# Third visit's keys and queries by DMA transposes, two score runs joined, and other places for copies and exponentials

## The chip, the cores and the metric

The kernel runs on one core of one Trainium2 chip. The metric is the device time of one execution in microseconds (us). The core has five engines that each work through their own instructions in order: TensorE (matmuls, PE in the profile; its weight loads are PEld), VectorE (DVE), ScalarE (ACT), GpSimd (POOL) and SyncE (SP, which here only issues DMAs). They wait for one another through semaphores.

## The reference

Attention in a sliding window, then a two-layer network on its output.

```python
scores = np.matmul(q, k.transpose(0, 1, 3, 2)) / np.sqrt(D)     # B, H, S, D = 8, 8, 576, 64
scores = np.where(np.abs(pos[:, None] - pos[None, :]) <= 32, scores, -1e9)
attn = softmax(scores)
x = np.matmul(attn, v).transpose(0, 2, 1, 3).reshape(B * S, H * D)   # 4608 x 512
h = x @ w_in                                                          # 512 x 2048
g = h * (1.0 / (1.0 + np.exp(-1.702 * h)))
out = g @ w_out                                                       # 2048 x 512
```

Inputs and output are float32; the kernel computes in bf16 and f16 with sums in float32.

## The kernel before, in words

The 4608 rows are cut into 36 units of 128 queries, and four units make a tile of 512 rows; there are nine tiles, 0 to 8. The queries of a unit are shifted by 32 rows, so that a block of 64 queries meets exactly 128 keys. All the code is written in one order by hand; every engine takes its own instructions from that order.

**A unit** goes through these steps: GpSimd issues the loads of keys, queries (`load_kq`, lines 137 to 143) and values (`load_v`, 208 to 213); keys and queries are transposed, either by TensorE with a copy out of the accumulator (`T_pe`, 242 to 251) or by a DMA that SyncE issues (`T_dma`, 236 to 240, called by `turn`, 811 to 813); `scores` (267 to 284) multiplies in 64x64 parts of the array and takes exponentials on ScalarE; `band` (308) multiplies the mask in on VectorE; `values` (316) multiplies with the values; `norm` (335) divides on VectorE; `x_T` and `x_T2` (385 to 410) transpose the result for layer 1. `odd_v` (218) copies values to a second buffer whose rows are shifted by 64; it runs on GpSimd. There are 9 buffers of values, 5 shifted ones, 5 each of untransposed keys and queries, and 7 each of transposed ones from unit 8 on.

**A tile** then goes through two layers. For tile 0 both are done in the plain way (`layer1_plain`, 477, and `layer2_plain`, 569: 32 matmuls of 512 columns for its first half). The others use Strassen's scheme with seven products (`l1_group`, 512 to 549, four groups a tile, counted 0 to 3; `layer2`, 597), whose sums of weights, inputs and gelus are made by VectorE (`w1_sums`, `w2_sums`, `x_sums`, `g_sums`, `g0_sum`). In `l1_group` the products 1, 7, 6, 2, 5, 4, 3 follow one another; line 537 and line 543 are the two VectorE sums between them that TensorE waits for, line 532 and 533 are the ScalarE copies, and line 524 is the gelu.

**Layer 2 as filler.** Layer 2 of a tile is a list, `self.l2` (also `more`), of single matmuls; `do(list, n)` takes the next n of them. So layer 2 of one tile fills the gaps in layer 1 and in the attention of the next ones. `fill(i)` in `first_layer1` (958 to 981, layer 1 of tile 1) says how many stand behind product i, and how many of the VectorE sums in `dv` are issued there; `side` does the same between products. `l2eng` is the engine that copies finished parts of layer 2's output, `seed2` the one that copies its starting sums.

**The order around the change.** `opening` (662 to 787) does units 0 to 7 and layer 1 of tile 0. The gelu needs another function table on ScalarE than the exponential. In the opening, some results of layer 1 are therefore kept aside by VectorE (`kept`) and their gelus deferred (`later=gelus`); line 743 takes one exponential of a single column, which makes ScalarE load the exponential's table there. Then come `x_sums(1)`, `first_layer1` with the transpose visits of units 8 to 12 (`T_pe` at its groups 1, 2, 3), and in `run` (905 to 947) the attention of units 8 to 15 among the items of layer 2. `back(2)` (847) starts layer 1 of tile 2.

**Queues.** All loads go through GpSimd's queue in order, stores of outputs (line 558) and DMA transposes through SyncE's. An instruction that waits holds up what is behind it on its engine.

Of the kernel before, what the change touches and what calls it, by code (L numbers as in the profile page):

```python
# [26 lines left out]
class _Kernel:  # L27
# [186 lines left out]

    def odd(self, u):
        return self.vo[u % 5 if u < 16 else (2, 3, 4, 0)[u % 4]]
# [14 lines left out]
    def place(self, c, u):  # L231
        t = self.sb(c + "T", [128, 4, 128], BF16, 7)
# [34 lines left out]
    def scores(self, u, tag):  # L267
# [15 lines left out]
        for eo in range(2):  # L283
            self.nc.scalar.activation(p[:, eo].rearrange("k h s -> k (h s)"), sc[eo], AF.Exp, scale=self.scale)  # L284
# [22 lines left out]

    def band(self, u, eng=None):
# [3 lines left out]
        pv = p.rearrange("p e (h b) s -> p (e h) b s", b=2)  # L312
# [41 lines left out]
    def values_four(self, u):  # L354
# [5 lines left out]
        for tag in self.FOUR:  # L360
            lo, n, pad = self.four(tag)
            for i in range(n):
                x, h = divmod(lo + i, self.H)
                at, more = pad + i * (D + 1), pad * (i == 0)
                for blk in range(2):
                    vt = (self.ve[(u + x) % 9], self.odd(u + x))[blk].rearrange("p h d -> p (h d)")
                    self.mm(self.acc[u][tag][64 * blk:64 * blk + 64, at - more:at + D + 1],
                            p[x][:, h % 2, h // 2 * 2 + blk, :], vt[:, h * (D + 2) - more:h * (D + 2) + D + 1],
# [200 lines left out]
    def layer2_plain(self, t, pr):  # L569
# [3 lines left out]
        def part(i, f):  # L573
# [5 lines left out]
            if f == 15:  # L579
                self.copy((self.nc.vector, self.nc.scalar)[i * pr], st["o"][:, i, :], st[i])  # L580
# [81 lines left out]
    def opening(self):  # L662
# [72 lines left out]
        l1(0, 8)  # L735
# [4 lines left out]
        l1(0, 10)  # L740
        l1(1, 8)
        self.T_four("q", "tA", (dve, act))
        act.activation(self.spark, self.spark, AF.Exp)
        gelus = []
        kept = [self.sb("s7", [128, 512], F32, 2)]
        room = self.sb("xs", [128, 2, 512], F32, 1, "room")
        kept += [room[:, i, :] for i in range(2)]
# [147 lines left out]
    def run(self):  # L895
# [20 lines left out]
        do(more, 4)  # L916
# [8 lines left out]
        do(more, 8)  # L925
# [102 lines left out]
```

## Time and profile before

| what | us |
| --- | --- |
| median of 3 runs | 279.58 (279.38 to 279.86) |
| the profiled execution | 279.59 |
| its span, first instruction to last | 277.8 |
| TensorE busy | 266.3 |
| VectorE busy | 212.1 |
| ScalarE busy | 197.3 |
| GpSimd busy | 138.6 |

The granted TensorE clock was 1.0 throughout. The time that runs show is 1.8 us more than the span, which lies ahead of the first instruction and behind the last. In the rows of a timeline stand the start and the duration in us from the span's start, the engine, the line, the operation, its output and inputs, the shape and type, how many instructions were merged (x8), and in brackets how long the engine stood idle before and what released it. Matmuls overlap, so the distance between starts says more than a duration. Line 70 is the helper that issues every matmul and line 67 the one that issues every copy; they are told apart by their tiles: `h` is layer 1, `o` layer 2, `sc` scores, `pv` values, `tp` a transpose. `kst` and `qst` are untransposed keys and queries, `kT` and `qT` transposed ones.

### The profile page before, as it was taken

What the parts mean: (1) busy time and instruction counts of PE and PEld (TensorE: products, weight loads), DVE (VectorE), ACT (ScalarE), POOL (GpSimd) and SP (SyncE); (2) the same over time, 40 slices, a digit from 0 to 9 for tenths busy, and PEclk for the clock granted to TensorE, in tenths of its full rate; (3) what the DMA queues carried; (4) which work ended last, traced back from release to release, by engine and by line L of the source; (5) the groups of instructions that cost most, each with busy time, mean ns of one, the idle gap of its engine ahead of it and who ended that gap; (6) DMA issues with size and microseconds to landing.
All of it is one profiled execution on the core that took longest, in us unless ns stands there. A gap on an engine that the chain in (4) does not pass through costs nothing.

```text
span 277.8 us, 8904 instructions
## 1 busy us (share of the span) xinstructions
PE 266.3 (96%) x3652; PEld 224.8 (81%) x3652; DVE 212.1 (76%) x487; ACT 197.3 (71%) x346; POOL 138.6 (50%) x216
## 2 busy tenths in 40 slices
PE   1989999999999999999999999999999999999994
PEld 1668656888888888888888888888888888888883
DVE  3455898897899788878888887888798878855631
ACT  2586896989896689568966895698569856577420
POOL 8895597999592089729641974294430000000000
PEclk9999999999999999999999999999999999999999
DMA  8999999999999999999999999999992024202033
GB/s 86 166 206 195 178 207 168 170 150 164 139 162 189 155 121 153 174 176 166 188 178 153 130 172 148 163 145 139 136 136 77 2 82 74 76 2 76 2 113 117
DMA packets 150809, 37.74 MB, mean 136 GB/s; under 512 B 138608, under 2 KB 146416, under 8 KB 150768
## 3 DMA queue, kind: packets, MB, share of 16 engines
q0 software_dynamic: 106656, 18.42, 96.4%
q1 hardware_dynamic: 43664, 18.23, 38.0%
q8 instruction: 28, 0.46, 0.7%
q10 hardware_dynamic: 448, 0.52, 0.6%
q14 instruction: 13, 0.11, 0.1%
HBM read 36.83 MB, written 9.44 MB: 167 GB/s over the span
## 4 chain that ended last, share of the span: by engine, by line
PE 91%; DVE 4%; ACT 2%; issue 1%; POOL 1%; POOLq 0%; DVEq 0%
PE o L70 40%; PE h L70 39%; PE sc L70 5%; PE pv L70 4%; PE tp L179 1%; PE tp L203 1%; POOL kq L154 1%; ACT p L284 1%; DVE xn L345 1%; PE tp L409 0%; PE tp L249 0%; DVE b L433 0%; DVE o_sb L67 0%; PE tp L397 0%; ACT kq L67 0%
## 5 line engine op out<-in xcount | busy, mean ns | idle before, releaser
L524 ACT ACTIVATE g<-h 128x512 f16<-128x512 f32 x128 | 72.2, 599 | 37.9 <-PE h L70 31.6
L70 PEld LDWEIGHTS <-g 128*128 128x128 f16 x568 | 54.6, 98 | 8.1
L70 PE MATMUL h<-xs,a 128*128 128x256 f16 x384 | 57.6, 272 | 0.3 <-DVE h L537 0.3
L70 PEld LDWEIGHTS <-a 128*128 128x128 f16 x512 | 49.7, 97 | 8.8 <-issue 0.6
L70 PEld LDWEIGHTS <-w 128*128 128x128 f16 x496 | 47.6, 98 | 7.7
L70 PE MATMUL h<-xT,w 128*128 128x256 f16 (+1 forms) x368 | 53.6, 277 | 0.1
L70 PE MATMUL o<-w,g 128*128 128x256 f16 (+1 forms) x304 | 49.8, 284 | 0.0
L70 PEld LDWEIGHTS <-gs 128*128 128x128 f16 x416 | 39.7, 98 | 5.5 <-issue 0.2
L227 POOL COPY vo<-ve 64x264 int32<-64x264 int32 x71 | 35.1, 494 | 16.4 <-DMA ve<-in_v_dram 10.0
L70 PE MATMUL o<-b,gs 128*128 128x256 f16 x280 | 43.3, 273 | 0.0
L70 PE MATMUL o<-b,g 128*128 128x256 f16 x264 | 38.5, 273 | 0.0
L213 POOL DMA_DIRECT2D ve<-in_v_dram x40 | 34.1, 860 | 5.4 <-DMA w<-in_moe_w_out_dram 1.8
L537 DVE TENSOR_TENSOR h<-h,s 128x512 f32<-128x512 f32 x32 | 22.3, 698 | 18.3 <-PE h L70 18.2
L284 ACT ACTIVATE p<-sc 128x512 bf16<-128x512 f32 x64 | 32.6, 619 | 1.1 <-PE sc L70 1.0
L143 POOL DMA_DIRECT2D qst<-in_q_dram x35 | 28.2, 807 | 1.7 <-issue 1.6
L543 DVE TENSOR_TENSOR h<-h,s 128x512 f32<-128x512 f32 x32 | 22.3, 698 | 7.6 <-PE h L70 7.4
L143 POOL DMA_DIRECT2D kst<-in_k_dram x31 | 26.4, 854 | 0.6 <-DMA qst<-in_q_dram 0.4
L67 ACT COPY h<-h 128x512 f32<-128x512 f32 x32 | 18.8, 589 | 10.4 <-PE h L70 9.8
L886 POOL COPY seen<-gs 1x1 f16<-1x1 f16 x17 | 3.3, 196 | 39.3 <-DVE gs L456 39.3
L314 DVE TENSOR_TENSOR p<-p,mask 128x1024 bf16<-128x1024 bf16 x32 | 21.8, 699 | 0.7 <-ACT p L284 0.7
L67 ACT COPY o_sb<-o 128x256 f32<-128x256 f32 (+1 forms) x24 | 11.1, 462 | 12.8 <-PE o L70 12.8
L67 ACT COPY s<-h 128x512 f32<-128x512 f32 x32 | 19.2, 600 | 0.8
(94 smaller groups left out, 377.8 us busy)
## 6 DMA issues: line engine op xcount, KB each, us to landing
out_dram<-o_sb SPq DMA_DIRECT2D x33, 256.0 KB, 3.8
ve<-in_v_dram POOLq DMA_DIRECT2D x32, 128.0 KB, 6.3
kst<-in_k_dram POOLq DMA_DIRECT2D x25, 128.0 KB, 6.0
qst<-in_q_dram POOLq DMA_DIRECT2D x21, 128.0 KB, 5.7
w<-in_moe_w_out_dram POOLq DMA_DIRECT2D x4, 512.0 KB, 11.1
w<-in_moe_w_in_dram POOLq DMA_DIRECT2D x3, 512.0 KB, 9.3
qst<-in_q_dram POOLq DMA_DIRECT2D x7, 96.0 KB, 6.0
kq<-in_q_dram POOLq DMA_DIRECT2D x2, 256.0 KB, 6.0
```

The source lines that it names most:

```text
L67: (eng.copy if eng is self.nc.scalar else eng.tensor_copy)(out, in_)
L70: self.nc.tensor.matmul(out, lhsT, rhs, start=start, stop=stop, skip_group_check=True)
L143: self.nc.gpsimd.dma_start(t[off:off + n], src[b, :, s:s + n, :].rearrange("h s d -> s h d"))
L154: self.nc.gpsimd.dma_start(self.stage["first"][0:n // j, :, at:at + j], src[0, :, lo:lo + n, :].rearrange("h (p j) d -> p h j d", j=j))
L213: self.nc.gpsimd.dma_start(t[off:off + n, :, :self.D], self.v[b, :, s:s + n, :].rearrange("h s d -> s h d"))
L227: eng.tensor_copy(*((words(vo[64:128]), words(self.ve[u % 9][64:128])), (words(vo[0:64]), words(nxt)))[i])
L284: self.nc.scalar.activation(p[:, eo].rearrange("k h s -> k (h s)"), sc[eo], AF.Exp, scale=self.scale)
L314: (eng or self.nc.vector).tensor_mul(pv, pv, msk.to_broadcast([128, 8, 2, SQ]))
L524: act.activation(g[:, f, 256 * half:256 * half + 256], bank.rearrange("p (i n) -> p i n", i=2), AF.Gelu_apprx_sigmoid)
L537: dve.tensor_add(e, b, s7)
L543: dve.tensor_add(c, b, s7)
L886: self.nc.gpsimd.tensor_copy(self.seen, self.gs[t - (n == 0)][0:1, 2, c, 255:256])
```

## The change

Keys 11, 12 and query 11 are transposed by DMAs that SyncE issues at group 1 of `first_layer1`, behind tile 1's first transpose visit, and the third visit goes. Queries 12 and 13 get one common tile. Units 4 and 5, and 12 and 13, have their scores in one run each (`scores_two`), as units 0 to 3 have already, without the starting bias. In `run`, the scores of unit 10 follow those of 9 at once, and one of unit 10's two exponentials is issued later; units 10 and 11 share a transpose. The opening takes whole-width products in place of half ones for the second half of layer 1, defers one gelu more, and loads the exponential's table before the second transpose of tile 1. Unit 8's values come in two loads; those of units 13 to 16 are issued together at group 3 in place of one in each group. The copies of tile 0's layer-2 output go to ScalarE. The counts of layer 2's items and of sums per fill are redistributed.

```diff
@@ kq_tile @@
-                self.qT[4 * t + i] = q[:, :, 128 * i:128 * i + 128]
+                self.qT[4 * t + i] = q[:, :, 128 * i:128 * i + (128 if i else 256)]
@@ new, beside load_v @@
+    def load_half(self, u, at):
+        b, s = divmod(128 * u + at, self.S)
+        self.nc.gpsimd.dma_start(self.ve[u % 9][at:at + 64, :, :self.D],
+                                 self.v[b, :, s:s + 64, :].rearrange("h s d -> s h d"))
@@ place @@
+        if c == "q" and u in (12, 13):
+            if u % 2 == 0:
+                self.qT[u] = self.sb("q_two", [128, 4, 256], BF16, 1)
+            return self.qT[u - u % 2][:, :, 128 * (u % 2):128 * (u % 2) + 128]
@@ scores @@
-    def scores(self, u, tag):
+    def scores(self, u, tag, hold=False):
...
-        for eo in range(2):
-            self.nc.scalar.activation(p[:, eo].rearrange("k h s -> k (h s)"), sc[eo], AF.Exp, scale=self.scale)
+        exps = [lambda eo=eo: self.nc.scalar.activation(p[:, eo].rearrange("k h s -> k (h s)"), sc[eo], AF.Exp,
+                                                         scale=self.scale) for eo in range(2)]
+        self.do(exps, 1 if hold else 2)
+        return exps
@@ new, behind scores_pair @@
+    def scores_two(self, u, tags):
+
+        k, q = [self.kT[u + i] for i in range(3)], self.qT[u]
+        sc = [x for tag in tags for x in self.score_banks(tag)]
+        for hp in range(4):
+            c = 256 * (hp % 2)
+            for eo in range(2):
+                r = slice(64 * eo, 64 * eo + 64)
+                for i in range(5):
+                    lo, hi = max(0, 64 * (i - 1)), min(256, 64 * (i + 1))
+                    rows = slice(64 * (i % 2), 64 * (i % 2) + 64)
+                    self.mm(sc[2 * (hp // 2) + eo][rows, c + lo:c + hi], k[i // 2][r, hp, rows], q[r, hp, lo:hi],
+                            start=c == 0 and i < 2)
+        self.pp = self.sb("p", [128, 2, 2, 8, SQ], BF16, 2)
...
+        for x in range(2):
+            for eo in range(2):
+                self.nc.scalar.activation(p[:, eo, x].rearrange("k y b s -> k (y b s)"), sc[2 * x + eo], AF.Exp,
+                                          scale=self.scale)
@@ layer2_plain @@
-                self.copy((self.nc.vector, self.nc.scalar)[i * pr], st["o"][:, i, :], st[i])
+                self.copy(self.nc.scalar, st["o"][:, i, :], st[i])
@@ opening @@
-        for u in (5, 6, 7, 8):
+        for u in (5, 6, 7):
             self.load_v(u)
+        self.load_half(8, 0)
...
-        l1(0, 8)
+        l1(None, 8)
...
-        l1(0, 10)
-        l1(1, 8)
+        l1(None, 9)
+        gelus = []
+        room = self.sb("xs", [128, 2, 512], F32, 1, "room")
+        kept = [self.sb("s7", [128, 512], F32, 2) for i in range(2)] + [room[:, i, :] for i in range(2)]
+        l1(None, 10, later=gelus, kept=kept[0])
+        act.activation(self.spark, self.spark, AF.Exp)
         self.T_four("q", "tA", (dve, act))
-        act.activation(self.spark, self.spark, AF.Exp)
...
-        l1(1, 10, later=gelus, kept=kept[0])
+        l1(None, 11, later=gelus, kept=kept[1])
...
+        self.load_half(8, 64)
         self.load_kq("k", 8)
...
-        self.scores(4, "AC")
-        self.scores(5, "t")
-        l1(None, 12, later=gelus, kept=kept[1])
+        self.scores_two(4, ("AC", "t"))
+        l1(None, 12, later=gelus, kept=kept[2])
         self.scores(6, "BE")
         self.band(4)
-        l1(None, 13, later=gelus, kept=kept[2])
+        l1(None, 13, later=gelus, kept=kept[3])
...
+        self.x_T2(4, "A", dve)
         self.w1_sums((2,), 1)
         self.g0_sum(0)
-        self.x_T2(4, "A", act)
@@ run @@
+        do(more, 6)
         self.scores(8, "t")
         self.scores(9, "AC")
+        exps = self.scores(10, "BE", True)
         self.turn(14)
         self.turn(15)
         do(late)
-        do(more, 20)
-        self.scores(10, "BE")
-        do(more, 12)
-        self.l2eng = dve
         self.band(8)
         self.band(9)
-        do(more, 4)
+        self.l2eng = act
+        do(more, 16)
+        do(exps)
+        do(more, 8)
         self.values(8, "t")
         self.values(9, "AC")
...
-        do(more, 8)
-        self.scores(12, "t")
-        do(more, 4)
+        do(more, 12)
+        self.scores_two(12, ("t", "BE"))
         self.values(10, "AC")
+        self.band(11)
         self.norm(10)
-        self.band(11)
-        self.scores(13, "BE")
         do(more, 8)
...
-        do(more, 4)
-        self.x_T(10, "A", dve)
-        do(more, 2)
-        self.x_T(11, "C", dve)
+        do(more, 6)
+        self.x_T2(10, "A", dve)
         self.scores(15, "t")
...
-        self.seed2 = dve
+        self.seed2 = self.l2eng = dve
@@ first_layer1 @@
-        extra = {0: [lambda: self.w1_sums((4,), 1), lambda: self.g0_sum(1)] + b((2, 0), (2, 1)), 1: b((4, 0), (4, 1)),
+        extra = {0: [lambda: self.g0_sum(1)] + b((2, 0), (2, 1)) + [lambda: self.w1_sums((4,), 1)], 1: b((4, 0), (4, 1)),
...
-            self.fetch(12 + n)
+            self.ahead("kq", 12 + n)
+            for u in ((), (), (), (13, 14, 15, 16))[n]:
+                self.load_v(u)
+
+            chunks = ((1, 2, 3, 3), (2, 2, 5, 4), (4, 4, 5, 4), (4, 4, 5, 4))[n]
+            sums = ((0, 0, 1, 1, 2), (2, 1, 1, 1, 2), (2, 1, 1, 1, 1), (2, 1, 1, 1, 1))[n]
 
             def fill(i):
-                self.do(self.l2, dict(zip((1, 7, 2, 4), ((1, 1, 3, 3), (1, 1, 3, 5), (2, 2, 8, 4), (2, 2, 6, 6))[n]))[i])
-                self.do(dv, {1: 2, 7: 1, 2: 0, 4: 2}[i] if n else {1: 0, 7: 1, 2: 0, 4: 1}[i])
-                if i == 7 and n:
-                    self.T_pe([("k8", "q8", "k9"), ("q9", "k10", "q10"), ("k11", "q11", "k12")][n - 1], self.nc.scalar)
+                at = (1, 7, 2, 4).index(i)
+                self.do(self.l2, chunks[at])
+                self.do(dv, {1: sums[0], 7: sums[1], 2: 0, 4: sums[4]}[i])
+                if i == 7 and n in (1, 2):
+                    self.T_pe((("k8", "q8", "k9"), ("q9", "k10", "q10"))[n - 1], self.nc.scalar)
+                if i == 7 and n == 1:
+                    for c, u in (("k", 11), ("q", 11), ("k", 12)):
+                        self.T_dma(c, u)
 
-            self.l1_group(1, n, fill, lambda i: self.do(dv, 1))
+            self.l1_group(1, n, fill, lambda i: self.do(dv, sums[2 + i]))
```

`band` and `values_four` only learn to read the exponentials of a joined run.

More of the change, by code (lines that the diff above doesn't have):

```diff
@@ L306, in scores_pair @@
                                           scale=self.scale)
+    def scores_two(self, u, tags):
[11 more added lines that the diff above has]
+        self.pp = self.sb("p", [128, 2, 2, 8, SQ], BF16, 2)
+        p = self.pp.rearrange("k e x (y b) s -> k e x y b s", y=2)
+        for i in range(2):
+            self.p[u + i] = p[:, :, :, :, 2 * i:2 * i + 2, :]
+        for x in range(2):
+            for eo in range(2):
+                self.nc.scalar.activation(p[:, eo, x].rearrange("k y b s -> k (y b s)"), sc[2 * x + eo], AF.Exp,
+                                          scale=self.scale)
     def band(self, u, eng=None):
@@ L311, in band @@
         a, b = 0 if cross[0] else 1, 2 if cross[1] else 3
-        pv = p.rearrange("p e (h b) s -> p (e h) b s", b=2)
+        pv = (p.rearrange("p e (h b) s -> p (e h) b s", b=2) if len(p.shape) == 4 else
+              p.rearrange("p e x y b s -> p (e x y) b s"))
         msk = self.mask[:, a:b + 1:b - a, :].rearrange("p (o b) s -> p o b s", o=1)
@@ L367, in values_four @@
                     self.mm(self.acc[u][tag][64 * blk:64 * blk + 64, at - more:at + D + 1],
-                            p[x][:, h % 2, h // 2 * 2 + blk, :], vt[:, h * (D + 2) - more:h * (D + 2) + D + 1],
+                            p[x][:, h % 2, h // 2 * 2 + blk, :] if len(p[x].shape) == 4 else
+                            p[x][:, h % 2, h // 4, h // 2 % 2, blk, :], vt[:, h * (D + 2) - more:h * (D + 2) + D + 1],
                             start=(i == 0))
```

4 lines of the change are left out of this document (removed).

## The prediction

> **What bounds the kernel now.** I read the page first: the share of each engine and the chain that ended last.
>
> ```profile
> PE 266.3 (96%) x3652; PEld 224.8 (81%) x3652; DVE 212.1 (76%) x487; ACT 197.3 (71%) x346; POOL 138.6 (50%) x216
> PE 91%; DVE 4%; ACT 2%; issue 1%; POOL 1%; POOLq 0%; DVEq 0%
> ```
>
> TensorE is busy for 266.3 of 277.8 us and carries 91% of the chain. A faster engine beside it gains nothing by itself. A change moves the end only if it takes work off TensorE, removes a place where TensorE stands still, or makes a new one. So I went through TensorE's timeline from the opening to the third tile's first product, which is where the diff lies, and compared each start with the start that the matmuls before it allow. Of these rows, the first two stand in group 2 of tile 1's layer 1, the next two in group 3.
>
> ```profile
> 56.63 1.04 PE L70 MATMUL o<-b,gs 128*128 128x256 f16 x8
> 57.92 0.60 PE L70 MATMUL h<-xs,a 128*128 128x256 f16 x4 [0.25 <-DVE h L537]
> ...
> 61.05 0.39 PE L249 MATMUL tp<-ident,kst 128*128 128x128 bf16 x4
> ...
> 61.72 0.60 PE L70 MATMUL h<-xs,a 128*128 128x256 f16 x4
> ```
>
> The next stretch is the end of that tile's layer 1 and the first score runs of `run`.
>
> ```profile
> 64.78 0.60 PE L70 MATMUL h<-xT,a 128*128 128x256 f16 x4
> 65.31 0.84 PE L70 MATMUL sc<-qT,kT 64*64 64x64 bf16 x48
> 66.08 0.61 PE L70 MATMUL o<-b,g 128*128 128x256 f16 x4
> ...
> 67.40 1.04 PE L70 MATMUL o<-w,g 128*128 128x256 f16 x8
> 68.37 0.45 PE L70 MATMUL sc<-qT,kT 64*64 64x64 bf16 x24
> 68.74 1.05 PE L70 MATMUL o<-w,gs 128*128 128x256 f16 x8
> ```
>
> The first column is the start. What counts is the distance from one start to the next, since durations overlap. Four matmuls of 256 columns and the step into a score run take 65.31 - 64.78 = 0.53; eight and the same step take 68.37 - 67.40 = 0.97. The difference gives **0.11 for a matmul** (0.44 for four) and about **0.09 for the step** from whole-array matmuls to 64x64 ones. A score run of 24 takes 68.74 - 68.37 = 0.37 to the next matmul.
>
> **The change, part by part.**
>
> *Keys and queries 11, 12 by DMA.* The third transpose visit goes: twelve TensorE transposes, 61.05 to 61.72, **-0.67 us**, all on the path, and three ScalarE copies, which were not. Three transposes are issued by SyncE instead. Their cost there is the slower rival below.
>
> *The layer-2 output copies of tile 0.* Both move from VectorE to ScalarE. After the eight matmuls from 56.63 the next could start at 57.51; it started at 57.92, 0.41 late, and waited for line 537 on VectorE.
>
> ```profile
> 53.74 0.68 DVE L67 COPY o_sb<-o 128x512 f32<-128x512 f32 x1
> ...
> 56.60 0.66 DVE L454 TENSOR_TENSOR g<-g 128x512 f16<-128x512 f16 x1
> 57.18 0.69 DVE L537 TENSOR_TENSOR h<-h,s 128x512 f32<-128x512 f32 x1
> ```
>
> Line 537 begins as soon as the sum before it ends, so VectorE is behind, not waiting. The two output copies (0.68 each, some 0.6 from start to start) are 1.2 of the queue ahead of it. Without them VectorE has more than the 0.41 in hand, also with the new order of the sums. **-0.41 us**. Something else may be late next: ScalarE takes the copies.
>
> ```profile
> 50.00:60.00 10.00, 9.75 (x96) 8.23 (x94) 8.97 (x18) 8.70 (x19) 9.80 (x16) 1.00 2.04 174
> ```
>
> In this ten-us stretch (columns: PE, PEld, DVE, ACT, POOL busy) ScalarE had 8.70; 1.2 more makes 9.9. It is full, but a product has about a microsecond between its copy and its use (fills stand between), so I take no wait. Bounds: 0 and +0.4.
>
> *Score runs joined.* `run` had seven runs of scores or values before the third tile; it will have five: unit 10 joins 8 and 9, and 12 and 13 go together ahead of values 10. Each run costs a step in and a step out. The step out follows from the opening's run of 48 below: 0.63 to the next matmul, against 0.37 for 24, so 24 scores cost 0.26 and the step out 0.11. Two runs: 2 x (0.09 + 0.11) = **-0.40 us**. That the 8, 9 run took 66.08 - 65.31 = 0.77 where 0.63 was due is a wait of 0.14 that the later start removes: **-0.14** (bounds 0 and 0.14). The joined form has 40 matmuls for 48 but as many columns; from nothing to 8 x 0.01 each, I take nothing.
>
> ```profile
> 30.69 1.01 ACT L67 COPY kq<-tp 128x1024 bf16<-128x1024 bf16 x1 [0.45 <-PE tp L203]
> 31.73 1.28 ACT L743 ACT_TABLE_LOAD   x1
> 33.02 0.20 ACT L743 ACTIVATE spark<-spark 128x1 f32<-128x1 f32 x1
> 33.13 4.00 ACT L284 ACTIVATE p<-sc 128x512 bf16<-128x512 f32 x8
> ```
>
> ```profile
> 31.76 0.70 PE L70 MATMUL sc<-kq 64*64 64x64 bf16 x48
> 32.39 1.04 PE L70 MATMUL h<-xT,w 128*128 128x512 f16 x4
> ```
>
> *The opening.* The table load (1.28) goes ahead of the copy at 30.69. The gelu that stood just ahead of that copy is now deferred, so the load fits into that room and the copy starts within 0.1 of where it was; the scores at 31.76, which need it, move by as much. The exponentials then start some 0.5 after the scores, at 32.3, in place of 33.13: 0.8 sooner. But the joined scores of 4 and 5 fill their banks across both units, so the mask of unit 4 needs all four exponentials (32.3 + 1.5 + 0.6 = 34.4), where it needed two (33.13 + 0.5 + 0.6 = 34.2). What TensorE gains behind units 5 and 6 it loses in front of unit 4, and VectorE, which gets a fourth kept copy and one transpose copy, sets the rest as before. **0**, bounds -0.3 and +0.3.
>
> *The exponentials of unit 10, held back.* Here a wait is added, and it is the largest unknown. The rows are ScalarE's behind the last gelus of tile 1.
>
> ```profile
> 65.07 1.11 ACT L524 ACTIVATE g<-h 128x512 f16<-128x512 f32 x2
> 66.19 1.28 ACT L284 ACT_TABLE_LOAD   x1
> 67.49 3.05 ACT L284 ACTIVATE p<-sc 128x512 bf16<-128x512 f32 x6
> 70.37 0.65 ACT L67 COPY o_sb<-o 128x512 f32<-128x512 f32 x1
> ```
>
> Call T the end of layer 1 of tile 1 on TensorE; before, T = 64.78 + 0.44 = 65.22. The two gelus ran back to back and ended at 66.18, T + 0.96. The last matmul ends at 64.78 + 0.60 = T + 0.16, and a gelu takes 0.6, so T + 0.76 is the earliest; I take 0.9. The load adds 1.3. Six exponentials take 3.05, a step of 0.49. In the new order five of them run (2.43), then the copy of layer 2's output that was at 70.37 (0.65), then the sixth (0.62). Scores 11 need the bank that the sixth empties: 0.9 + 1.3 + 2.43 + 0.65 + 0.62 = **T + 5.9**. TensorE gets there sooner than before, because six layer-2 matmuls are now behind T's other side: 30 matmuls (3.3), one run of 72 scores (0.09 + 0.26 x 3 + 0.11), values 8 and 9 with their steps (0.7) = **T + 5.0**. So it stands **0.9 us**, partly ahead of values 9, whose mask needs the exponentials of unit 9. Behind this wait on TensorE is everything, as it is one queue. Bounds: 0.6 (gelu at T + 0.76, and steps for durations) and 1.2; 0 if TensorE itself is that much later.
>
> A rule of the Trainium skill speaks against bringing the exponentials onto the path: "ScalarE: Activation LUTs", section "What ACT_TABLE_LOAD costs", has about 1.28 us for the load and about 1.38 more for a drain, 2.66 together. The trace disagrees on the drain: the load starts at 66.19, right behind the gelu that ends at 66.18, and the first exponential at 67.49, so 1.3 in all.
>
> *After scores 11.* The transposes of 10 and 11 become one visit with one copy; the sums behind it need that copy.
>
> ```profile
> 71.23 0.45 PE L70 MATMUL sc<-qT,kT 64*64 64x64 bf16 x24
> ...
> 78.39 0.60 PE L70 MATMUL h<-xT,w 128*128 128x256 f16 x4
> ```
>
> ```profile
> 77.44 0.87 DVE L67 COPY xT<-tp 128x512 f16<-128x512 f16 x2
> ```
>
> These two copies, 0.87 together, now both stand behind unit 11's transposes. From nothing to +0.4 for the sums; I take **+0.1**. The split load of unit 8's values and the later loads of 13 to 16 are GpSimd's; their users are many microseconds on, and I take nothing for them.
>
> Sum: -0.67 - 0.41 - 0.40 - 0.14 + 0.9 + 0.1 = **-0.6**; I add -0.2 for the other short waits on line 543 and in the value runs of this stretch, which have the same causes (bounds 0 and -0.4). **-0.8 us**. From tile 2 on TensorE has no gap of size and the code is the same, so the gain is carried to the end. The profiled execution took 279.59 (span 277.8 and 1.8 around it), and the median of the runs shown is 279.58, so no correction: **278.8 us**.
>
> **The rivals.**
>
> *B, no stand at scores 11.* If ScalarE's chain and TensorE's meet nearer to each other than I placed them, the 0.9 goes: 279.59 - 1.7 = 277.9. For it: both ends of the 0.9 are sums of many terms, and TensorE's end may be later. Against it: a load and six exponentials can't be made shorter. Chance 0.20.
>
> *C, the wait only moves.* ScalarE at 9.9 of 10 in groups 1 and 2 makes the copies of a product late, so that the 0.41 stays, and the opening loses 0.1: 278.8 + 0.5 = 279.3, no measurable change. For it: the stretch's row. Against it: ScalarE loses three transpose copies one group later. Chance 0.19.
>
> *D, slower: SyncE's queue.* Unit 15's scores need key 16.
>
> ```profile
> 50.25 0.92 POOL L143 DMA_DIRECT2D kst<-in_k_dram  x1
> ```
>
> ```profile
> 59.06 1.29 SPq L240 DMA_TRANSPOSE qT<-qst  x1
> ...
> 72.83 1.19 SPq L240 DMA_TRANSPOSE kT<-kst  x1
> ```
>
> ```profile
> 77.78 0.45 PE L70 MATMUL sc<-qT,kT 64*64 64x64 bf16 x24
> kst<-in_k_dram POOLq DMA_DIRECT2D x25, 128.0 KB, 6.0
> ```
>
> Eight transposes go through SyncE from 59.06 to 72.83, in order, and the last must land within 77.78 - 72.83 = 4.95 to cause no wait. Three more, of 1.2 to 1.3, now stand ahead of them, with tile 0's stores behind them. Key 12 is issued at 50.25 and needs 6.0, so its transpose can start at 56.3 and be out by 57.6, ahead of 59.06; and the value loads that stood between the later keys go behind key 16. That is against it. For it: the transposes share the DMA engines with the loads, and a late key 12 delays all eight. It decides once key 16 is issued later than 77.0 - 4.95 = 72.05; each further transpose's length costs 1.25, all three give 278.8 + 0.8 + 3.75 = 283.3, one gives 280.8. Chance 0.10.
>
> *E, a switch that costs twice its load.* If ScalarE must also empty itself at the switch, for as long as the load once more (1.28), the chain to scores 11 is that much longer: 280.1. Since 66.18 to 66.19 shows no such time, chance 0.03. By the 1.38 of the Trainium skill's section above it would be an estimated 280.2.
>
> **How the numbers follow.** My forecast has 0.48, with a range of its own from 278.3 to 279.1. About 0.2% (0.56 us) is what a measurement here can tell from no change, so faster means below 279.0 and slower above 280.1. Faster: nearly all of the forecast (0.45) and B (0.20), 0.65. Same: C and the rest, 0.22. Slower: D and E, 0.13. The range runs from 277.8, which takes in most of B, to 280.1, and leaves D out.
>
> **What the new profile would show.** Right: no transposes of key 11 and 12 on TensorE; the wait on line 537 near 57 gone; five runs of 64x64 matmuls from unit 8 to 15; TensorE idle some 0.5 to 0.9 just ahead of or inside values 9 and scores 11, released by line 284 (the exponentials); the third tile's first product near 77.6 in place of 78.39. Wrong: that wait missing (B), or a wait of the same size on ScalarE's copies near 55 to 58 (C), or scores 11, 12 or 15 released by a DMA transpose (D).

## The result, and the profile after

| | before | changed |
| --- | --- | --- |
| median of 16 runs each, us | 279.63 (279.23 to 281.02) | 280.79 (279.82 to 283.71) |
| ratio, 95% interval | | 1.0051 (1.0028 to 1.0075) |
| the profiled execution | 279.59 | 280.64 |
| its span | 277.8 | 278.9 |

The change made the kernel **slower by 0.5%**; 278.8 was forecast. (Medians and ranges here are of all executions; the ratios leave disturbed ones out.) On the page, TensorE is busy for 264.4 us, 1.9 less than before, and its share of the chain fell from 91% to 86%:

```profile
PE 264.4 (95%) x3608; PEld 221.4 (79%) x3608; DVE 211.5 (76%) x485; ACT 195.4 (70%) x345; POOL 140.0 (50%) x217
PE 86%; DMA 6%; ACT 4%; POOL 1%; DVE 1%; issue 1%; POOLq 0%
```

So work was taken off TensorE, and the time went to standing still. (The 6% for DMA in the chain is not this. It is two loads at the very start, of queries from 4.22 on and of weights up to 20.56; before, the chain goes through the engines there, and TensorE is only 0.17 sooner behind it, at 20.44 in place of 20.61.) TensorE's timeline of the changed kernel shows first what the prediction had asked for; "a stand" is a time in which TensorE stands idle with work left to do:

```profile
57.81 0.71 PE L70 MATMUL o<-b,gs 128*128 128x256 f16 x5
58.40 0.60 PE L70 MATMUL h<-xs,a 128*128 128x256 f16 x4
...
66.00 0.95 PE L70 MATMUL sc<-qT,kT 64*64 64x64 bf16 x72
66.88 1.05 PE L70 MATMUL o<-w,g 128*128 128x256 f16 x8
...
69.86 0.19 PE L70 MATMUL pv<-vo,p 128*64 128x65 bf16 x1
70.23 0.22 PE L70 MATMUL pv<-ve,p 128*64 128x65 bf16 x1 [0.18 <-DVE p L348]
...
70.60 0.78 PE L70 MATMUL sc<-qT,kT 64*64 64x64 bf16 x24
71.31 1.05 PE L70 MATMUL o<-b,gs 128*128 128x256 f16 x8
...
77.47 0.39 PE L70 MATMUL o<-b,gs 128*128 128x256 f16 x2
77.94 0.60 PE L70 MATMUL h<-xT,w 128*128 128x256 f16 x4
78.38 0.38 PE L70 MATMUL o<-b,gs 128*128 128x256 f16 x2
79.39 0.61 PE L70 MATMUL h<-xs,a 128*128 128x256 f16 x4 [0.63 <-DVE xs L476]
```

Five matmuls take 58.40 - 57.81 = 0.59, so the wait on the old line 537 (now 572) is gone. The run of 72 scores takes 0.88 (0.89 was worked out). The new stand behind the exponentials is there: 0.37 between two value matmuls where a step costs some 0.13, and 0.71 for scores 11 where 0.37 is due, 0.24 and 0.34, 0.58 together. Tile 2 begins at 77.94, 0.45 sooner than at 78.39. Then, in code that the change doesn't touch, two matmuls that take 0.22 are followed by a pause: the next product starts 1.01 later. The view names line 476 on VectorE as the releaser, but that sum had ended at 78.35. A view names the last semaphore as the releaser; where that had long come, as here, something else was late.

Five marks cut the executions into pieces: A, B, C are the starts of the first product of tiles 1, 2 and 3, E that of TensorE's last matmul, S SyncE's last check of a store's semaphore.

| us | A | A to B | B to C | C to E | E to S |
| --- | --- | --- | --- | --- | --- |
| before | 43.47 | 34.92 | 26.07 | 169.51 | 2.94 |
| changed | 43.77 | 34.17 | 27.13 | 169.34 | 3.55 |
| difference | +0.30 | **-0.75** | **+1.06** | -0.17 | **+0.61** |

The differences make +1.05, and so do the two times (280.64 - 279.59). Between the starts of tiles 1 and 2 the gain came as predicted, 0.75 for 0.8. It is given back, and more, behind it (1.06 and 0.61) and ahead of it (0.30).

### The profile page after: what moved, and what is told of

It reads as the page before. It is cut to its first block, busy times and chain, and to the rows that moved or that the text cites. A ratio compares the mean times of both kernels' runs of the same rounds, so it can differ in the third digit from the quotient of the medians.

```text
span 278.9 us, 8814 instructions
## 1 busy us (share of the span) xinstructions
PE 264.4 (95%) x3608; PEld 221.4 (79%) x3608; DVE 211.5 (76%) x485; ACT 195.4 (70%) x345; POOL 140.0 (50%) x217
## 4 chain that ended last, share of the span: by engine, by line
PE 86%; DMA 6%; ACT 4%; POOL 1%; DVE 1%; issue 1%; POOLq 0%
PE h L70 39%; PE o L70 39%; DMA w<-in_moe_w_in_dram 3%; PE sc L70 3%; PE pv L70 3%; DMA kq<-in_q_dram 2%; ACT p L292 1%; POOL kq L154 1%; ACT kq L67 1%; PE tp L444 1%; ACT g L559 1%; PE tp L258 0%; ACT L292 0%; ACT L781 0%; DVE xs L476 0%
## 5 line engine op out<-in xcount | busy, mean ns | idle before, releaser
L70 PEld LDWEIGHTS <-w 128*128 128x128 f16 x480 | 45.9, 98 | 9.6 <-DMA w<-in_moe_w_in_dram 0.7
L213 POOL DMA_DIRECT2D ve<-in_v_dram x39 | 33.1, 862 | 2.5 <-DMA w<-in_moe_w_in_dram 1.3
L292 ACT ACTIVATE p<-sc 128x512 bf16<-128x512 f32 x56 | 28.9, 622 | 0.4 <-PE sc L70 0.2
L67 ACT COPY o_sb<-o 128x256 f32<-128x256 f32 (+1 forms) x27 | 12.7, 470 | 12.6 <-PE o L70 12.6
```

The source lines that it names most:

```text
L67: (eng.copy if eng is self.nc.scalar else eng.tensor_copy)(out, in_)
L70: self.nc.tensor.matmul(out, lhsT, rhs, start=start, stop=stop, skip_group_check=True)
L213: self.nc.gpsimd.dma_start(t[off:off + n, :, :self.D], self.v[b, :, s:s + n, :].rearrange("h s d -> s h d"))
L292: exps = [lambda eo=eo: self.nc.scalar.activation(p[:, eo].rearrange("k h s -> k (h s)"), sc[eo], AF.Exp, scale=self.scale) for eo in rang ...
```

## The experiments

Each time stands beside runs of the kernel before on the same chip, and each ratio is to those. F is the theory that TensorE's own instructions come late: the profile has a DMA queue q8, instruction, with packets of 16 KB, and each packet begins when TensorE has passed another 256 rows, or up to some us after it (matmuls, weight loads and TensorE's semaphore instructions counted together). Q is that the transposes by DMA come late; S is the prediction's sum as it stands. Other letters are explained where they stand.

### The same kernel again, and rows shifted

e1 is the changed kernel unaltered. e2 is the changed kernel, e3 the kernel before, with 32 and 64 matmuls of one column on zeros (two rows each) ahead of everything, where TensorE waits for its first keys; nothing else differs.

```diff
         self.setup()
+        self.dummy = self.cst.tile([128, 8], BF16, name="dummy")
+        dve.memset(self.dummy, 0.0)
+        pad = self.bank("E", name="pad")
+        for i in range(32):
+            self.mm(pad[0:1, 0:1], self.dummy[:, 0:1], self.dummy[:, 0:1], start=True, stop=True)
```

> The changed kernel once more. Theory F (TensorE's instructions come in blocks of 256 by DMA, and in the dense stretch of scores and values a block comes too late): the profile again shows TensorE idle at the same instruction, near 78.5 us, with no engine to blame, by 0.3 to 2 us, and a q8 packet that lands some 1.3 us ahead of the restart; times spread over 3 us as before. Rival Q (key 16's transpose is late in the slower runs): in a profile slower than 280.6 scores 14 or 15 are released by a DMA transpose. Rival S (only sizes of steps were wrong): no idle time beyond engine waits. Median 280.3 to 281.2 by all.

> The changed kernel with 32 one-column matmuls on zeros in TensorE's first idle microseconds: 64 instructions more, so every block boundary moves 64 instructions earlier in the code; nothing else changes. Theory F: boundaries then stand at 72.4 and 98.9 us of the old trace, with only 4.7 and 5.0 us from one to the next where a fetch took up to 6.3: 1 to 2.5 us slower than the changed kernel, and idle time at the new boundaries, none at the old one. Q and S: within 0.3 us of the changed kernel.

> The kernel before with 64 such matmuls, 128 instructions. Theory F: one block then covers 70.6 to 74.2 us, 3.6 us in place of the 4.4 at most that any block had: 0.5 to 2.4 us slower than before, idle near 74.2. Q and S: within 0.3 us of the kernel before.

Measured: e1 280.74, ratio 1.0058 (1.0045 to 1.0071); e2 281.67, 1.0089 (1.0077 to 1.0102); e3 280.20, 1.0040 (1.0028 to 1.0052). Rows that cost nothing where they stand cost each kernel 0.8 to 0.9 us. The profile of e3 shows where: in the middle of one run of scores, between two matmuls that wait for no semaphore.

```profile
74.11 0.40 PE L70 MATMUL sc<-qT,kT 64*64 64x64 bf16 x19
75.34 0.25 PE L70 MATMUL sc<-qT,kT 64*64 64x128 bf16 x5 [0.83 <-issue]
```

"issue" as releaser means that the engine waited for nothing that the profile shows. Here are all such stands of 0.3 or more behind the first 10 us, in all kernels that have one, with the packets of q8 that land ahead of them:

| kernel | packet | TensorE goes on | later by | stand |
| --- | --- | --- | --- | --- |
| changed | 77.01 to 78.05 | 79.39 | 1.34 | 0.8 |
| e2 | 77.38 to 78.51 | 79.91 | 1.40 | 1.6 |
| e2 | 13.82 to 15.07 | 16.48 | 1.41 | 2.2 |
| e3 | 72.72 to 73.92 | 75.34 | 1.42 | 0.8 |
| e7 | 75.92 to 76.90 | 78.27 | 1.37 | 1.3 |
| e1 | 32.62 to 34.03 | 35.46 | 1.43 | 0.5 |
| e5 | 33.42 to 34.36 | 35.83 | 1.47 | 0.8 |
| e10 | 34.17 to 35.12 | 36.56 | 1.44 | 0.6 |
| e11 | 33.95 to 34.89 | 36.39 | 1.50 | 0.9 |
| e11 | 71.96 to 73.12 | 74.59 | 1.47 | 0.3 |
| e17 | 32.79 to 34.12 | 35.47 | 1.35 | 0.5 |

In each the first row behind the stand is row 193 + 256 n of TensorE, or the one after it, and the matmul there starts 1.34 to 1.50 behind the packet's end. In no trace of this case is a block entered less than 1.29 behind its packet. That is what F asks for. Its size for e2 was a little high (1 to 2.5 over the changed kernel; 0.9 came), and part of e2's loss is not where F had looked: the stand at 16.48 lies in the opening, and tile 1 starts at 44.87 in place of 43.77. And e1 hadn't the stand at 78.4 and was no faster. Beside a stand at 35.46 it waited for something else, which is Q:

```profile
75.59 0.24 PE L70 MATMUL sc<-qT,kT 64*64 64x64 bf16 x2
76.29 0.44 PE L70 MATMUL sc<-qT,kT 64*64 64x64 bf16 x22 [0.46 <-DMA kT<-kst]
```

So what is late differs from one execution to the next, and both come by DMA.

### The third visit given back

```diff
-                if i == 7 and n in (1, 2):
-                    self.T_pe((("k8", "q8", "k9"), ("q9", "k10", "q10"))[n - 1], self.nc.scalar)
-                if i == 7 and n == 1:
-                    for c, u in (("k", 11), ("q", 11), ("k", 12)):
-                        self.T_dma(c, u)
+                if i == 7 and n:
+                    self.T_pe((("k8", "q8", "k9"), ("q9", "k10", "q10"), ("k11", "q11", "k12"))[n - 1], self.nc.scalar)
```

> The changed kernel with keys 11, 12 and query 11 transposed by TensorE at group 3 again, in place of the three DMA transposes. S: 0.67 us slower than the changed kernel. Q: SyncE's queue is short again, the slow runs go: 0.3 to 1 us faster than the changed kernel and a smaller spread. F: block boundaries move 24 instructions from group 3 on and three DMAs fewer stand ahead of the fetches: it can go either way by 1 us, with the idle time at another instruction.

Measured: 282.98, 1.0130 (1.0114 to 1.0145), far over the 0.67. In its profile scores 15 wait 1.74 for key 16, which lands at 79.37 in place of 76.34. The five value loads, still in one lump, start at 68.44 in place of 64.64, and key 16's transpose is issued at 72.70 in place of 69.77. That the visit frees the buffers of untransposed keys later, and so moves the loads back, is the likely reason; no run tested it. e4 undid a part of the change and not the order of the loads that goes with it; e12 does both.

### Fewer loads, another order, another opening

e5 leaves the loads of value rows 13 to 16 out of the changed kernel, e6 puts them back into the four groups:

```diff
-            for u in ((), (), (), (13, 14, 15, 16))[n]:
-                self.load_v(u)
```

```diff
-            self.ahead("kq", 12 + n)
-            for u in ((), (), (), (13, 14, 15, 16))[n]:
-                self.load_v(u)
+            self.fetch(12 + n)
```

e7 is the changed kernel with the old `opening`, e8 the kernel before with the new one; the main lines of e7 are

```diff
-        l1(None, 10, later=gelus, kept=kept[0])
-        act.activation(self.spark, self.spark, AF.Exp)
+        l1(0, 10)
+        l1(1, 8)
         self.T_four("q", "tA", (dve, act))
+        act.activation(self.spark, self.spark, AF.Exp)
...
-        self.scores_two(4, ("AC", "t"))
+        self.scores(4, "AC")
+        self.scores(5, "t")
```

> The changed kernel without its four loads of value rows 13 to 16 (0.5 MB, issued at 64.6 to 68.7 by GpSimd; units 13 to 16 then use older rows, so part of the output is not the reference's). Every instruction of TensorE is in its old place. Theory F (TensorE's own instructions, and the keys' transposes, are late because their packets stand behind the loads in the DMA engines): the instruction packet asked for at about 73.1 comes within 2.5 us in place of 3.8 to 3.9, keys 15 and 16 land before 75, TensorE has no stand of over 0.4 us between 74 and 80, and the time is 279.6 to 280.2 (about 0.8 below the changed kernel's 280.8). Theory L (the loss was made by TensorE's, VectorE's and ScalarE's own work, in the opening and behind 97): the time stays within 0.3 of 280.8.

> The changed kernel with the loads of value rows 13 to 16 given back to the four groups, one behind each query and key load, as the kernel before had them; TensorE's instructions are unchanged. Theory F, with the order of the loads deciding: the instruction packet asked for at 73.1 waits under 2.5 us, the stand at 78.4 goes, time 279.8 to 280.4. Theory F, with the total deciding: the transposes of keys 15 and 16 come later by as much (after 76.5), TensorE waits for them instead, 280.5 to 281.3. Theory L: 280.8 within 0.3.

> The changed kernel with the opening of the kernel before (its order of layer 1, scores 4 and 5 apart, ScalarE's table load where it was). TensorE gets 48 instruction rows more ahead of the stretch. Theory O (the opening itself costs about 0.3 us, as 38.46 was reached 0.3 later in the profile): 280.4 to 280.6 if nothing else moves. Theory F: the 48 rows move the boundaries of the fetched blocks so that 256 rows are used up in 4.4 us from 72.8 to 77.2, a packet that takes 3.8 + 1.0 us and 1.3 more to be usable is late by 1 to 1.9 us there: 281.2 to 282.2, with an idle stretch of over 1 us between 76.5 and 79.

> The kernel before with the opening of the changed one alone. Theory O: 279.5 + 0.3 = 279.8. Theory F: TensorE gets 47 instruction rows fewer ahead of the stretch, so two blocks behind one another (68.4 to 72.8 and 72.8 to 77.9) are used up in 4.4 and 5.1 us, with stands of 0.3 to 1 us in each: 280.3 to 281.3, idle in the middle of runs of scores or values, where no semaphore is waited for. Prediction's step (opening at no cost, bounds -0.3 to +0.3): 279.2 to 279.8.

e5: 279.77, 1.0017 (1.0005 to 1.0030), a full us below the changed kernel, as F said. (Its profiled execution, 280.32, is one of its slower ones and has a stand of 0.8 in the opening.) The packet began 0.8 behind its crossing (the passing of the 256 rows) in place of 3.9, keys 15 and 16 landed at 72.2 and 73.5 in place of 74.8 and 76.3, and TensorE passes the place of the stand without one:

```profile
78.41 0.60 PE L70 MATMUL h<-xT,w 128*128 128x256 f16 x4
78.84 0.38 PE L70 MATMUL o<-b,gs 128*128 128x256 f16 x2
79.06 0.60 PE L70 MATMUL h<-xs,a 128*128 128x256 f16 x4
```

The view of the DMA queues between 64 and 78 shows the reason. Each digit is the busy share of the 16 DMA engines in 0.35 us; here is the changed kernel, and behind it e5:

```profile
DMA  9999999999999999999999971999999997999200
```

```profile
DMA  9999999999999999999008909607999100002999
```

The engines of the changed kernel have next to no room up to 77; those of e5 have some from 70.6 on. (The kernel before has hardly more room than the changed one. Key 16 lands at 76.45 there and at 76.34 in the changed kernel, but the scores that need it start at 77.78 there and at 77.09 here.)

e6: 280.70, 1.0051 (1.0035 to 1.0067): the second of the two outcomes under F, though not by keys. The block's packet waited 2.0 and no key was late, but behind tile 3's start the inputs of layer 1, transposed by DMA, were:

```profile
106.66 0.50 PE L70 MATMUL h<-xs,a 128*128 128x256 f16 x3 [0.87 <-DVE xs L476]
```

```profile
106.18 0.42 DVE L476 TENSOR_TENSOR xs<-xT 128x512 f16<-128x512 f16 x1 [1.72 <-DMA xT<-xn]
```

e7: 280.82, 1.0077 (1.0046 to 1.0108). F named the stand and its place; it is 1.34, inside a run of scores (281.2 to 282.2 was too much):

```profile
76.63 0.30 PE L70 MATMUL sc<-qT,kT 64*64 64x64 bf16 x8
78.27 0.38 PE L70 MATMUL sc<-qT,kT 64*64 64x64 bf16 x16 [1.34 <-issue]
```

e8: 279.97, 1.0027 (1.0016 to 1.0038). The opening alone is a small loss; F had asked for 280.3 to 281.3, and its stands aren't in the profile: the two blocks were entered 3.3 and 2.3 behind their packets, where some 1.3 is enough.

### The middle part alone

e9 has the old opening and the loads of e6, so that the runs, the copies and the third visit's transposes by DMA are what is left. e10 is e9, and e11 is e7, with 88 of the dummy matmuls; e12 is e9 with the edit of e4 (visit on TensorE).

> The changed kernel with the old opening (as in e7) and with the loads of value rows 13 to 16 one behind each query and key load (as in e6): of the change only its middle part is left. Theory F (TensorE's instruction block comes late behind the loads): the block asked for at 72.3 waits some 2 us in place of 3.6, the stand of 1.34 at 76.7 falls under 0.3, and the time is 279.4 to 279.9. If the middle part itself is no gain: 280.5 to 281.

> As e9, with 88 one-column matmuls on zeros ahead of everything on TensorE, in its idle first 5 us: 176 instruction rows, so that no block boundary falls between 73 and 79 and the short blocks are 30.0 to 35.1 and 67.6 to 73.0. Theory F: no stand with the releaser issue behind 40; tile 2 starts before 77.7 and the time is 279.0 to 279.6, the least of all. If added rows cost by themselves (64 and 128 rows added 0.9 and 0.8): 280.2 to 280.8.

> As e7 (old opening, the changed kernel's loads), with the same 176 rows ahead. The loads still delay every packet by 3 to 4 us, but no boundary falls where 256 rows pass in under 5.3 us behind 70. Theory F: the stand of 1.34 at 76.7 is gone, 279.3 to 279.9; keys 15 and 16 land at 75.3 and 75.9 against scores at 75.1 and 76.6 less 0, so up to 0.5 may come back as a wait for them. If added rows cost by themselves: 281.2 to 281.8.

> As e9, with the third transpose visit of TensorE back (k11, q11, k12) and their DMA transposes gone: what is left of the change is the joined runs, the copies on ScalarE and the order of the chunks. Prediction's step 1 (the visit is worth 0.67 of TensorE, the transposes by DMA cost nothing): e9 + 0.6 to + 0.8. Rival (three transposes more on loaded DMA engines cost about what the visit did): e9 within 0.3. Theory F's caution: the visit's 24 rows move the boundaries, 0.5 either way.

What F expected of the times of e9 to e11 failed: e9 281.27, 1.0073 (1.0048 to 1.0098); e10 281.56, 1.0071 (1.0048 to 1.0095); e11 283.9, 1.0116 (1.0081 to 1.0150). e9 has no stand for instructions, as F said, but a wait of almost the same size for key 15:

```profile
75.18 0.24 PE L70 MATMUL sc<-qT,kT 64*64 64x64 bf16 x2
76.41 0.44 PE L70 MATMUL sc<-qT,kT 64*64 64x64 bf16 x22 [0.98 <-DMA kT<-kst]
```

e10 lost 0.6 to a block at 36.6 and 0.2 to query 15, e11 0.9 at 36.4 and 0.3 at 74.6 to blocks and 1.8 to the inputs of layer 1 at 107.9. **e12: 280.11**, 1.0024 (1.0005 to 1.0043), 1.2 *below* e9 with twelve transposes more on TensorE. So F alone is too narrow: it is one of three ways in which the same load is paid for: late instruction blocks, late keys and queries, and late inputs of layer 1.

### The square

What was open is whether the gain for the engines was right where the DMA engines have room. e13 is the kernel before, e14 is e9, e15 is e12, each without the loads of value rows 13 to 16 (units 13 to 16 then use older rows). e16 is the kernel before with the one edit of `layer2_plain`, its copies on ScalarE.

```diff
-            self.fetch(12 + n)
+            self.ahead("kq", 12 + n)
```

> The kernel before without its loads of value rows 13 to 16 (units 13 to 16 use older rows; part of the output is not the reference's). Theory Q (the DMA engines between 56 and 78 are what the change overloads; the kernel before has no wait for them): 279.2 to 279.5, no change. Rival (these loads cost any kernel about 1 us, so e5 told nothing of the change): 278.2 to 278.6.

> As e9 (middle part alone, third visit by DMA) without the loads of value rows 13 to 16 (work left out as in e13). Theory Q: keys 15 and 16 land before scores 14 and 15, no wait on a DMA between 70 and 80, and the gain that the prediction worked out for the engines shows: 278.4 to 279.0. If the engines' gain was wrong as well: 279.3 or more.

> As e12 (middle part with the third visit on TensorE) without the loads of value rows 13 to 16. With e14 it gives what the visit is worth where the DMA engines have room. Prediction's step 1: e14 + 0.6 to + 0.8, so 279.1 to 279.7. Theory Q: the same, while with the loads the order is the other way round (e12 below e9 by 1.2). If the transposes by DMA cost by themselves, loads or not: e15 below e14.

> The kernel before with the one edit that the first two copies of layer 2's output go to ScalarE (no DMA and no row of TensorE is moved). Prediction's step 2: the wait of 0.25 to 0.41 at 57.9 goes and is carried on: 278.9 to 279.2. Rival (something later takes it back, the keys' transposes above all, which do not come sooner): 279.4 to 279.6, with a new wait of 0.2 to 0.4 on a DMA or on VectorE before 80.

| third visit | with the loads | without them | A to E without, profile |
| --- | --- | --- | --- |
| by DMA | e9 281.27 | e14 279.34 (1.0000, 0.9987 to 1.0013) | 229.67 |
| on TensorE | e12 280.11 | e15 279.35 (0.9999, 0.9991 to 1.0008) | 230.31 |
| kernel before | 279.4 | e13 279.63 (1.0010, 1.0001 to 1.0019) | 230.66 |

The loads cost the kernel before nothing, e12 0.8 and e9 1.9. Without them TensorE's part of e14 up to tile 2 is what the prediction had: tile 2 begins at 77.53 (77.6 was foreseen), and it is passed without a pause.

```profile
77.53 0.60 PE L70 MATMUL h<-xT,w 128*128 128x256 f16 x4
77.97 0.38 PE L70 MATMUL o<-b,gs 128*128 128x256 f16 x2
78.19 0.60 PE L70 MATMUL h<-xs,a 128*128 128x256 f16 x4
```

From A to B e14 takes 34.18, e15 34.85: 0.67, the predicted worth of the visit to the hundredth. Yet its time is no lower than that of before: 278.4 to 279.0 was expected, and 279.34 falls under the other outcome. So that the gain for the engines was right is shown by one profile, and not by the times.

e16: 279.20, 1.0003 (0.9987 to 1.0019), nothing that can be measured in the time. In its profile the eight matmuls ahead of the old wait take 56.88 to 57.75, 0.87 in place of 1.29, so the 0.42 is gone. But a layer-2 matmul at 53.16 now waits for ScalarE's copy that ends at 53.10, and the five matmuls there take 0.83 in place of 0.65. From A to B 34.68 is left for 34.92, a gain of 0.24. (From A to E e16 is 0.43 shorter than before's 230.50, but 0.21 of that lies behind C, where e8, with the same code there, differs from before by 0.24.)

### The end, and a version of its own

In e14 the way from E to S is 3.35, in e15 2.97, in before 2.94. What SyncE waits for at the end tells why; first before, then the changed kernel (the columns are the total, the number of waits and the longest):

```profile
SPq L1023 <- DMA out_dram<-o_sb: 1.9, 4, 0.7
```

```profile
SPq L1064 <- DMA out_dram<-o_sb: 2.8, 1, 2.8
```

SyncE checks eight DMA semaphores one behind the other, 0.06 from one to the next; DMAs are given to them in turn. In the kernel before the last store signals the sixth (116): by then five checks are done, and two follow, 276.79 to 276.91. Three DMAs more turn the last store to the first (111): seven follow, 277.54 to 277.96. That is 0.30 us. All kernels so far with the third visit by DMA end on 111, all others on 116. e17 is the changed kernel with five transfers of 256 bytes more, at the start of SyncE's queue; e18 is e7 with the loads of value rows 15 and 16 and their copies (`odd_v` 14 and 15) moved behind the load of query 16 and of key 17, and seven such transfers.

```diff
+        tiny = self.cst.tile([1, 5, 64], F32, name="tiny")
+        for i in range(5):
+            self.nc.sync.dma_start(tiny[:, i, :], self.q[0, 0, i:i + 1, :])
```

> The changed kernel with five transfers of 256 bytes from q into an unused tile, issued by SyncE at the very start, where it has nothing to do for 50 us. Theory E (SyncE checks its eight DMA semaphores one behind the other at the end, 0.06 each; three DMAs more turned the last store from the sixth to the first): the last store signals 116 again, two checks stand behind it in place of seven, and the time is 0.31 lower: 280.4 to 280.6. Rival (the checks are hidden or the order does not follow the count): 280.7 to 280.9, or the profile shows seven checks behind the last store still.

> Nothing left out: the middle part of the change alone (old opening), the loads of value rows 15 and 16 behind those of query 16 and key 17 (at 77 in place of 67) with their two copies in the next tile, and seven tiny transfers, so that the last store signals 118, the last to be checked. Theory: key 15 and key 16 land before 76, no stand of over 0.4 between 70 and 80, TensorE's stretch from the second tile's layer 1 to its end as in e14 (229.7) and no checks behind the store: 278.8 to 279.2 against 279.4 of before. Rival (the moved loads delay query 16 to key 20, or values of unit 12 wait for unit 15's copy at 88): 279.6 to 280.6 with a wait on a DMA or on POOL between 85 and 105.

e17's profile shows 116 again, and two checks behind it (277.48 to 277.60); its profiled execution took 280.31. The median was 281.21 (279.85 to 282.62), 1.0063 (1.0041 to 1.0085), above both ranges that were expected and with a spread in which 0.3 can't be seen, so the price stands on the rows alone. e18 failed: 285.4, 1.0176 (1.0134 to 1.0217). Key 15 was late by 0.68 all the same, and the moved loads met the transposes of layer 1's inputs:

```profile
108.10 0.61 PE L70 MATMUL h<-xs,a 128*128 128x256 f16 x4 [1.70 <-DVE xs L476]
```

No version was found that beats the kernel before.

## Why the prediction was wrong, point by point

- **Third visit, -0.67.** Right for TensorE (0.67 between e14 and e15). **This is the step that failed: "Three transposes are issued by SyncE instead", with their cost put off to a rival, and then "the code is the same, so the gain is carried to the end".** The three transposes and the earlier loads ask for time on DMA engines that are busy in nearly every slice from 56 to 77, and TensorE arrives sooner at things that do not come sooner. Behind tile 2's start the gain of 0.75 was lost again: 1.06 up to tile 3 and 0.61 at the end. e9 against e12 gives the price of the transposes by DMA: +1.2 where -0.67 was forecast; without the four value loads, e14 against e15, it is 0.0 in the time. The price depends on the order of the loads: in the changed kernel itself, where the value loads stand in one lump, giving the visit back to TensorE (e4) cost another 2.2.
- **The wait on line 537, -0.41.** Right for the wait: gone in the changed kernel, and 0.42 shorter in e16. There 0.18 came back as a wait for ScalarE's copies, which rival C had named, and what was left, 0.24, can't be seen in e16's time.
- **Runs joined, -0.40 and -0.14.** Right as far as it shows: 0.88 for 72 scores against 0.89.
- **Opening, 0 with 0.3 either way.** A comes 0.30 later in the changed kernel, but 0.17 of that stands at 20.61 already, behind a wait of 0.58 for weights that e9, e13 and e16, with the old opening, have as well (0.88, 0.67, 0.72). e8 puts the opening at +0.27% (0.16 to 0.38), which is 0.4 to 1.1 us and outside the bounds; no single wait in e8's profile carries it, so its cause stays open.
- **Stand behind the exponentials, +0.9.** 0.58 was found, just below the lower bound of 0.6. Its two places were right (ahead of values 9, inside scores 11).
- **One transpose for 10 and 11, +0.1.** 77.47 to 77.94 is 0.47 for two matmuls, so 0.25, within the bounds.
- **The sum up to tile 2, -0.8.** -0.75 from tile 1's start, and -0.45 with the opening (77.94, where near 77.6 was foreseen). That -0.75 fits so closely is in part luck, since two terms were off in opposite ways (0.58 for 0.9, 0.25 for 0.1) and the -0.2 for other short waits was not checked by itself. From there on it isn't the sum of the engines' work that counts.
- **Rival D** came nearest: key 15 or 16 was late in e1, e4, e9 and e18. But it looked at the queue of issues, and its condition (key 16 issued later than 72.05) did not hold: in the changed kernel it was issued at 69.77 and took 6.6 to land where 4.95 was allowed. What is short is not SyncE's time but the DMA engines'.
- **What no rival had.** TensorE's own instructions. In the changed kernel 256 rows from 73.1 on were used up in 5.4 us. Their successor's packet began 3.9 later, took 1.0 and was usable 1.3 after that. In e5, with room on the DMA engines, it began after 0.8. The Trainium skill, "Runtime: NRT & Kernel Launch", section "Instruction fetch mechanics", says that a sequencer fetches blocks of 16 KiB, 256 instructions, by a DMA queue of its own while it works through the one before, and calls the cost mostly hidden. The size agrees with the packets here; hidden it was not, by 0.3 to 2.2 us a time.
- **The rest of the loss.** The 1.06 from B to C is the stand of 0.8 and one of 0.3 at 98.25, where line 572 on VectorE starts 0.4 behind the check that its input is there (97.08 and 97.50). e1, e5, e6 and e17, with the same instructions on VectorE, have it at the same row, its 192nd, and each time a packet of 8 KB on queue q14, instruction, starts 0.7 to 1.2 later; that it is VectorE's own block boundary is likely, but no run was made to show it. Of the 0.61 behind E, 0.30 is the checks; the rest is the last store, which landed 2.4 after its issue in place of 2.1.

Open stays how the loss divides among the three kinds of late arrivals, since it does so anew in each execution, and why the end of TensorE's work, 0.96 sooner in e14's profile, became 0.1 in the median (279.34 for 279.4): 0.4 goes to the end, and the profiled execution, at 279.06, was one of its fastest.

## What to carry to other kernels

Where the DMA engines are busy in every slice, a transpose moved from TensorE to DMA need not be free, even if its own result comes in time: price it by what else must arrive there, instruction blocks among them. And a shorter way on one engine gains only up to the next thing that comes by DMA at its own time; look for the slack of each such arrival before carrying a gain to the end. A change of 0.3% can't be told from where the 256-instruction boundaries happen to fall (64 and 128 rows more cost 0.9 and 0.8 us here): shift them with a few dummy instructions before believing it.

## What the runs showed of the hardware beyond that

- The stands for instructions came where 256 rows, scores and value matmuls among them, passed in 4.4 to 6.8 us, and the packet began 2.0 to 5.4 behind the boundary before, took 0.9 to 1.4 and was usable 1.3 to 1.5 after that.
- The time from issue to landing of a key's transpose depends on the loads beside it: issued between 65 and 72, three took 4.5, 4.4 and 2.3 in e5, without the value loads, and two 5.4 and 8.1 in e1.
- Three DMAs more turned the last store to another semaphore, and the end of the kernel was 0.30 longer for it.
